# Attention and channel mixing on one core: x as the stationary operand of the token mix, the query scale inside the row maximum, weight conversion's last addition on VectorE

## The chip, the cores and the metric

The kernel runs on one core of one Trainium2 chip. The metric is the device time of an execution in microseconds (us), lower is better; a kernel's time is the median of its runs. Engine names are those of the profile: PE is the matrix engine's multiplications and PEld its loads of stationary operands, DVE is VectorE, ACT is ScalarE, POOL is GpSimd, and SP only issues transfers.

## The reference

```python
# attention: q, k, v are (4 batches, 8 heads, 576 rows, 64); tau = 0.02
scores = q @ k.T / sqrt(64)
thresh = max(scores, -1) - tau
scores = where(scores >= thresh, scores, -1e9)
attn   = exp(scores - max(scores, -1))
attn   = attn / (sum(attn, -1) + 1e-9)
x      = attn @ v                       # heads side by side: (4, 576, 512)
# token mix (rank 32) and channel layers
h   = x.transpose(0, 2, 1) @ U @ V      # U (576, 32), V (32, 576)
u   = x + h.transpose(0, 2, 1)
x   = u + relu(u @ w_ch1) @ w_ch2       # w_ch1 (512, 2048), w_ch2 (2048, 512)
# gated convolution over rows, 5 taps
gate = sigmoid(sum_k conv_w[k] * x shifted by 4 - k rows)
out  = (gate * (x @ w_val)) @ w_out
```

The weights arrive as 64-bit floats; the kernel reads them as pairs of 32-bit words and converts them itself.

## The kernel before, in words

**Precision.** A product that must be as good as 32-bit is made of three products of a faster type: an operand is split into a high part (a copy on ACT) and a low part (a subtraction on DVE or POOL), and high x high, high x low and low x high are summed. Transposes and the products with the values and with U stay in plain 32-bit, in which one product is issued as two instructions.

**Attention: 16 pairs of heads, nine slots each.** A head has 576 rows, four tiles of 128 and a tail of 64. The two tails of a pair share slot 0, the eight tiles are slots 1 to 8. The loop over s in `attention` issues in every slot: `soft_max` (DVE, one pass over the scores in PSUM that writes their negatives `ns` and takes their minimum `nm`), `soft_exp` (ACT, and a one-column sum `th` on POOL), `soft_mask` of the slot before (DVE: keeps what is above the threshold and sums it), then on PE the scores of the next slot (`scores`, two buffers in PSUM) and the transposes of the slot before the last (`trans_main`, `trans_tail`), whose results ACT copies out. `pv` multiplies by the values (twice in a pair), `back` transposes the result back, and a DVE multiplication by 1/sum writes x into `ring`. `mix_t` then makes t = x^T U, `mix_u` and `mix_ut` make u = x + t V. `prep_T` and `stacks` prepare q and k of the next pair. What ACT and DVE do with a PE result is put off with `later(slot, place)`: place 0 and 1 come before `soft_exp`, 2 and 3 behind it. `ORDER` sorts the PE work of a slot, `LATE_ORDER` what is put off, `AT` and `PREP_AT` say in which slot of a pair a step falls.

In `mix_t` the stationary operand is `u4`, U repeated four times (128 columns), and x moves (128 columns), five products, so that t comes out four times one above the other (128 x 128); a copy and a subtraction in the lower half make the high and low parts.

**Weight conversion.** `from_f64` turns a 128 x 512 block into 32-bit in seven steps: absolute value (ACT), clamp, shift, merge, mask, scaled low word (DVE) and one last addition (POOL). The steps are generators; `Staged.tick` moves up to `width` blocks one step on, and each call of `tick` stands at a fixed place of the program. Ten blocks are converted during attention (U, V, and the first quarter of both channel weights, `chunk(0, 0)` and `chunk(0, 1)`), the rest between matrix products afterwards. The queue of each engine is in order: a step waits there and holds up what is behind it.

**After attention.** The first quarter of the channel layers runs straight (`h1`, `ch`, blocks of 512 rows). Beside it `combos` forms sums and differences of blocks of u in `ring`, splits them into three landing tiles in `c_sb` and writes them to DRAM. The other three quarters (c = 1 to 3) use a seven-product scheme: `first_layer` fetches seven operands from DRAM (`region`), multiplies them (lines 1163) and combines the results in `c_sb` on DVE (lines 1139, 1151, and 1134 for the low parts); `second_layer` (1201) adds into u (1204). The weights of the next quarter are combined on DVE (202) and split on ACT and POOL (208, 209) meanwhile. `val` and `proj` are the gated convolution's products and the output.

Of the kernel before, what the change touches and what calls it, by code (L numbers as in the profile page):

```python
# [36 lines left out]
def attention_moe_kernel(  # L37
# [15 lines left out]
    nc = tc.nc  # L53
# [44 lines left out]
    def from_f64(dst, t, raw, clp=0, lowp=0):  # L98
# [30 lines left out]
        nc.gpsimd.tensor_tensor(out=dst, in0=dst, in1=tf, op=ALU.add)  # L129
# [16 lines left out]
    def convert(raw, clp=0, lowp=0, into=None):  # L146
# [7 lines left out]
        yield from from_f64(w[0:m, 0:n], t[0:m, 0:n], raw, clp, lowp)  # L154
# [61 lines left out]
    class Staged:  # L216
# [21 lines left out]
        "pv": (8, 12), "back": 13, "t": 15, "u": 18, "lq": 0, "lv": 4, "uv": 4, "ch": 10,  # L238
    }

    PREP_AT = {"Tq": (-3, 0), "Tk": (1, 1), "Tt": (2, 2), "stA": (4, 4), "bd": (4, 4), "stB": (5, 5)}

    ORDER = {
        "mix_t": 4, "mix_u": 3, "mix_ut": 5, "next_scores": 0, "prep_T": 5, "pv": 3, "back": 2,
        "trans_main": 2, "trans_tail": 2,
    }
    LATE_ORDER = {
        "T": -2, "n": -1, "nt": -2, "o": -1, "t": 0, "u": 1, "x": -2,
    }

    CONVERT_AT = (0, 1, 6, 9, 12, 16)
# [14 lines left out]
    def attention(dense_front, dense_mid, dense_top, dense_left, dense_back):  # L266
# [15 lines left out]
        u4 = setup.tile([128, 5, 128], F32, name="u4")  # L282
# [24 lines left out]
        def load_qk(p):  # L307
            eng = nc.gpsimd if 1 < p < 4 else nc.sync
# [47 lines left out]
        def hi_lo_qk(p, nm, ps, a, n):  # L356
            qk = st8[p]["qk"]
            hi = qk[:, {"q": 0, "k": 1}[nm], a:a + n]
            lo = qk[:, {"q": 3, "k": 2}[nm], a:a + n]

            def act():
                if nm == "q":
                    nc.scalar.activation(out=hi, in_=ps, func=ACTF.Copy, scale=qscale[:, 0:1])
                else:
                    nc.scalar.activation(out=hi, in_=ps, func=ACTF.Copy)

            def dve():
                if nm == "q":
                    nc.vector.scalar_tensor_tensor(
                        out=lo, in0=ps, scalar=qscale[:, 0:1], in1=f(hi), op0=ALU.mult, op1=ALU.subtract  # L370
                    )
                else:
                    nc.vector.tensor_tensor(out=lo, in0=ps, in1=f(hi), op=ALU.subtract)

            return act, dve


        def hi_lo_q0(hh, dst, ps):
# [3 lines left out]
                lambda: nc.scalar.activation(out=hi, in_=ps[a], func=ACTF.Copy, scale=qscale[a, 0:1]),  # L382
                lambda: nc.vector.scalar_tensor_tensor(
# [919 lines left out]
```

## Time and profile before

| | |
|---|---|
| median of 3 runs | 816.7 us (813.84 to 816.81) |
| the profiled execution: time, span | 815.51 us, 813.7 us |
| PE, PEld busy, share of the span | 98%, 89% |
| DVE, ACT, POOL busy | 84%, 54%, 31% |
| granted clock of the matrix engine | 0.999 of full speed (2.4 GHz) |

Busy time of PE includes the modelled ends of pipelined products, so that a busy PE may still have been held up for a part of it; what the matrix engine issues is seen from the starts of its instructions. The span is cut below into startup (0 to 28 us), attention in its steady state (28 to 312), the first quarter of the channel layers (312 to 424), the other three (424 to 711) and the end.

### The profile page before, as it was taken

To read this page: it belongs to the slowest core of one execution; us is meant where nothing else is said; L and a number is where in the kernel's file an instruction comes from. 1 tells how busy PE (TensorE), PEld (TensorE's weight loads), DVE (VectorE), ACT (ScalarE), POOL (GpSimd) and SP (SyncE) were. 2 spreads that over 40 slices of the span, in tenths; PEclk is the share of its full clock that TensorE was granted. 3 is DMA by queue.
4 is the path that set the end of the run, shared out by engine and by line. 5 is a ranking of instruction groups with operands and counts; after the bars stand their busy time and mean duration, and the time that the engine had idled before them with its cause. 6 is when DMAs were issued, how large, how long until landed. Compare 5 with 4: busy or idle time off the path is not lost.

```text
span 813.7 us, 15121 instructions
## 1 busy us (share of the span) xinstructions
PE 798.9 (98%) x5264; PEld 721.0 (89%) x5264; DVE 680.1 (84%) x1426; ACT 442.1 (54%) x929; POOL 252.3 (31%) x350
## 2 busy tenths in 40 slices
PE   9999999999999999999999999999999999999998
PEld 8788888888888887888799998998999999988886
DVE  7999999999999997387989799588899898988740
ACT  6789888888898887343433225132243252355431
POOL 6723622632422331044353226311464230000000
PEclk9999999999999999999999999999999999999999
DMA  5666776685676443445768658277475573001112
GB/s 152 182 143 147 177 166 150 140 203 134 144 183 143 103 104 137 147 153 207 287 247 301 209 216 298 73 303 263 152 297 200 214 272 116 2 1 52 52 53 77
DMA packets 87397, 134.19 MB, mean 165 GB/s; under 512 B 45669, under 2 KB 62837, under 8 KB 87322
## 3 DMA queue, kind: packets, MB, share of 16 engines
q1 hardware_dynamic: 85130, 130.92, 52.7%
q0 software_dynamic: 848, 1.92, 0.8%
q8 instruction: 42, 0.69, 0.3%
q10 hardware_dynamic: 1344, 0.39, 0.2%
q14 instruction: 33, 0.27, 0.1%
HBM read 85.43 MB, written 21.23 MB: 131 GB/s over the span
## 4 chain that ended last, share of the span: by engine, by line
PE 81%; DVE 8%; DMA 4%; issue 2%; ACT 2%; POOL 1%; ACTq 0%; DVEq 0%; POOLq 0%; SPq 0%
PE s L469 9%; PE o L578 8%; PE c L1201 8%; PE a L1201 8%; PE xm L524 7%; PE v L913 6%; PE p L1101 6%; PE a L1163 5%; PE c L1163 5%; PE a L913 4%; PE c L913 3%; DMA region<-sp 2%; PE o L567 2%; PE t L617 2%; DMA sp<-c_sb 2%
## 5 line engine op out<-in xcount | busy, mean ns | idle before, releaser
L508 DVE SCALAR_TENSOR_TENSOR e<-ns,th,e 128x576 f32<-128x576 f32 x144 | 124.4, 864 | 1.5 <-POOL th L498 0.4
L498 POOL TENSOR_TENSOR th<-nm,scalars 128x1 f32<-128x1 f32 x144 | 70.2, 487 | 178.1 <-DVE ns L483 171.1
L497 ACT ACTIVATE e<-ns,nm 128x576 f32<-128x576 f32 x144 | 111.9, 777 | 20.4 <-DVE ns L483 20.3
L483 DVE TENSOR_SCALAR_CACHE_REDUCE ns<-s 128x576 f32<-128x576 f32 x144 | 107.7, 748 | 9.0 <-PE s L469 8.2
L129 POOL TENSOR_TENSOR wf<-wf,wt 128x512 f32<-128x512 f32 (+2 forms) x43 | 59.9, 1394 | 134.1 <-DVE wt L124 131.0
L469 PE MATMUL s<-st 128*128 128x288 f32 x480 | 94.0, 318 | 0.1
L524 PE MATMUL xm<-idn,e 128*128 128x128 f32 x576 | 86.6, 273 | 2.4 <-DVE e L508 2.4
L533 ACT ACTIVATE pt<-xm 128x512 f32<-128x512 f32 x144 | 85.7, 595 | 1.6
L1201 PE MATMUL a<-region,w 128*128 128x384 f32 x432 | 80.9, 334 | 1.0 <-DVE region L1134 1.0
L1201 PE MATMUL c<-region,w 128*128 128x384 f32 x432 | 80.7, 334 | 0.0
L1163 PE MATMUL a<-region,w_s 128*128 128x384 f32 x378 | 76.6, 337 | 2.9 <-DVE c_sb L1139 1.5
L469 PEld LDWEIGHTS s<-st 128*128 128x128 f32 x480 | 67.8, 189 | 11.9 <-issue 4.6
L1201 PEld LDWEIGHTS a<-region,w 128*128 128x128 f32 x432 | 75.3, 188 | 1.3 <-DVE region L1134 1.3
L1163 PE MATMUL c<-region,w_s 128*128 128x384 f32 x378 | 75.7, 334 | 0.0
L1201 PEld LDWEIGHTS c<-region,w 128*128 128x128 f32 x432 | 75.4, 188 | 0.0
L524 PEld LDWEIGHTS xm<-idn,e 128*128 128x128 f32 x576 | 69.4, 141 | 4.6 <-PE s L469 2.3
L1140 ACT ACTIVATE region<-c_sb 128x384 fp32r<-128x384 f32 x72 | 37.7, 525 | 64.6 <-DVE c_sb L1139 64.3
L1163 PEld LDWEIGHTS a<-region,w_s 128*128 128x128 f32 x378 | 65.8, 188 | 5.3 <-DVE c_sb L1139 3.1
L578 PE MATMUL o<-pt,vt 128*64 128x256 f32 (+1 forms) x768 | 69.8, 331 | 0.0
L1163 PEld LDWEIGHTS c<-region,w_s 128*128 128x128 f32 x378 | 66.4, 188 | 0.0
L578 PEld LDWEIGHTS o<-pt,vt 128*64 128x64 f32 x768 | 41.4, 137 | 24.4 <-issue 10.6
L172 ACT ACTIVATE w<-wf 128x512 fp32r<-128x512 f32 x28 | 17.7, 631 | 66.4 <-POOL wf L129 66.4
(164 smaller groups left out, 1555.7 us busy)
## 6 DMA issues: line engine op xcount, KB each, us to landing
region<-sp SPq DMA_DIRECT2D x63, 768.0 KB, 6.0
raw<-in_moe_w_ch_dram SPq DMA_DIRECT2D x32, 512.0 KB, 4.5
sp<-c_sb SPq DMA_DIRECT2D x24, 384.0 KB, 2.9
st<-qk SPq DMA_DIRECT2D x30, 256.0 KB, 3.4
st<-qk SPq DMA_DIRECT2D x15, 432.0 KB, 3.9
st<-qk SPq DMA_DIRECT2D x45, 144.0 KB, 3.9
out_dram<-c_sb SPq DMA_DIRECT2D x17, 256.0 KB, 2.0
st<-qk SPq DMA_DIRECT2D x15, 288.0 KB, 4.9
```

The lines of the kernel that those rows point to most:

```text
L129: nc.gpsimd.tensor_tensor(out=dst, in0=dst, in1=tf, op=ALU.add)
L469: nc.tensor.matmul(s[:, n, 0:HS], lhs, rhs[:, n * HS:(n + 1) * HS], start=(m == 0), stop=(m == len(ops) - 1))
L483: nc.vector.tensor_scalar(out=ns.rearrange("p (a b) -> p a b", a=2), in0=s, scalar1=-1.0, scalar2=3.0e38, op0=ALU.mult, op1=ALU.min, accum ...
L497: nc.scalar.activation(out=row(p, i), in_=d["ns", i], func=ACTF.Exp, bias=nm[:, 0:1], scale=-1.0)
L498: nc.gpsimd.tensor_tensor(out=th, in0=nm, in1=tau_eff, op=ALU.add)
L508: nc.vector.scalar_tensor_tensor(out=e, in0=d.pop(("ns", i)), scalar=d.pop(("th", i))[:, 0:1], in1=e, op0=ALU.is_le, op1=ALU.mult, accum_o ...
L524: nc.tensor.transpose(x[:, j * 128:(j + 1) * 128], e[:, c + j * 128:c + (j + 1) * 128], idn)
L533: later(s + 1, 0, lambda: nc.scalar.activation(out=dst, in_=x.rearrange("p (j c) -> p j c", j=4), func=ACTF.Copy), "x")
L578: nc.tensor.matmul(o, lhs, rhs, start=False, stop=stop)
L913: nc.tensor.matmul(ps[:, 0:m1], lhs, rhs, start=(m == 0), stop=(m == len(ops) - 1))
L1163: nc.tensor.matmul(ps, lhs, rhs, start=k == 0, stop=k == 5)
L1201: nc.tensor.matmul(ps, lhs, rhs, start=k == 0, stop=k == 3 * KD - 1)
```

## The change

- `mix_t`: x is the stationary operand and U (`u1`, 32 columns) moves; t comes out as 128 x 32. ACT copies it twice side by side, DVE subtracts it twice (128 x 64), a new step `mix_tt` transposes the four parts together on PE (128 x 128), and ACT copies the result to `t_st`.
- The query scale is no longer applied to q when its parts are made (plain copy and subtraction), but within `soft_max`: the factor there was the constant -1 and is now a per-partition operand, `qscale`, which holds -1/8.
- `from_f64`: after slot 144, the last addition is on DVE. U and V take their clamp and scaled low word on POOL and ACT and the addition on DVE; the first quarter of both weights takes the scaled low word on DVE (for w_ch1 it was ACT and POOL) and the subtraction for the low part on DVE.
- `soft_mask` moves ahead of the work that is put off; `th` of the first pair moves from POOL to DVE; loads of q and k of pairs 2 and 3 move from POOL's queue to SP's.
- Slots: `mix_t` 15 to 16, `mix_tt` 18, `mix_u` and `mix_ut` 18 to 20, `chunk(0, 0)` 10 to 6, `chunk(0, 1)` 10 to 110; `mix_t`, `mix_tt`, `mix_ut` and the tails' `pv` share a small PSUM tile. The tables of ticks change.
- `combos` has four landing tiles, and from its second third on its differences are on DVE. `fetch` takes free buffers from a list, with as many in flight as before.

```diff
-    def from_f64(dst, t, raw, clp=0, lowp=0):
+    def from_f64(dst, t, raw, clp=0, lowp=0, add=nc.gpsimd):
...
-        nc.gpsimd.tensor_tensor(out=dst, in0=dst, in1=tf, op=ALU.add)
+        (nc.vector if slot[0] > 9 * NP else add).tensor_tensor(out=dst, in0=dst, in1=tf, op=ALU.add)
...
-            eng = nc.gpsimd if 1 < p < 4 else nc.sync
+            eng = nc.sync
...
-                if nm == "q":
-                    nc.scalar.activation(out=hi, in_=ps, func=ACTF.Copy, scale=qscale[:, 0:1])
-                else:
-                    nc.scalar.activation(out=hi, in_=ps, func=ACTF.Copy)
+                nc.scalar.activation(out=hi, in_=ps, func=ACTF.Copy)
...
-                out=ns.rearrange("p (a b) -> p a b", a=2), in0=s, scalar1=-1.0, scalar2=3.0e38, op0=ALU.mult,
+                out=ns.rearrange("p (a b) -> p a b", a=2), in0=s, scalar1=qscale[:, 0:1], scalar2=3.0e38, op0=ALU.mult,
...
-            nc.gpsimd.tensor_tensor(out=th, in0=nm, in1=tau_eff, op=ALU.add)
+            (nc.gpsimd if p or 0 else nc.vector).tensor_tensor(out=th, in0=nm, in1=tau_eff, op=ALU.add)
...
-            x = xtile("t")[:, 0:128]
-            t, xs = t_st[p % 2], x_of(p)
+            x = xsmall(s)[:, 0:R]
+            t, xs = tt_sb[p % 2], x_of(p)
             for j in range(5):
-                nc.tensor.matmul(x, u4[:, j, :], xs[:, j, :], start=(j == 0), stop=(j == 4))
-            later(s + 1, 0, lambda: nc.scalar.activation(out=t, in_=x, func=ACTF.Copy), "t")
+                nc.tensor.matmul(x, xs[:, j, :], u1[:, j, :], start=(j == 0), stop=(j == 4))
+            both = x.unsqueeze(1).to_broadcast([128, 2, R])
+            later(s + 1, 1, lambda: nc.scalar.activation(out=t[:, 0:2, :], in_=both, func=ACTF.Copy), "t")
             later(s + 1, 3, lambda: nc.vector.tensor_tensor(
-                out=t[64:128], in0=x[64:128], in1=f(t[64:128]), op=ALU.subtract
+                out=t[:, 2:4, :], in0=both, in1=f(t[:, 0:2, :]), op=ALU.subtract
             ), "t")
+
+        def mix_tt(s, p):
+            x = xsmall(s)[:, 0:128]
+            nc.tensor.transpose(x, f(tt_sb[p % 2]).rearrange("p g r -> p (g r)"), idn)
+            later(s + 1, 2, lambda: nc.scalar.activation(out=t_st[p % 2], in_=x, func=ACTF.Copy), "t")
...
-            w = yield from convert(raw_uv[part])
+            w = yield from convert(raw_uv[part], 1, 1, nc.vector)
...
-            if s == AT["ch"]:
-                chunk(0, 0)
-                chunk(0, 1)
-            work.width = 2 if s < 9 * NP - 11 else 4
+            if s == 6: chunk(0, 0)
+            if s == 110: chunk(0, 1)
+            work.width = 2 if s < 9 * NP - 9 else 4
...
-                    if 1 <= s <= 9 * NP:
-                        soft_mask(*divmod(s - 1, 9))
+                if m == 1 and live:
+                    soft_exp(p, i)
+                if m == 0 and 1 <= s <= 9 * NP:
+                    soft_mask(*divmod(s - 1, 9))
...
-              nc.vector if c == 0 and part else nc.gpsimd,
-              *((0, 1) if c == 0 and not part else ())))
+              (nc.vector if part else nc.vector) if c == 0 else nc.gpsimd,
+              *(((0, 0, nc.gpsimd) if part else (0, 0, nc.gpsimd)) if c == 0 else ())))
...
-        outs = [p1["c"][:, 2 * n * G:2 * (n + 1) * G].rearrange("p (a n) -> p a n", a=2) for n in range(3)]
+        outs = [p1["c"][:, 2 * n * G:2 * (n + 1) * G].rearrange("p (a n) -> p a n", a=2) for n in range(4)]
...
-            (nc.vector if j > 1 else nc.gpsimd).tensor_tensor(out=lots[i % 3], in0=x, in1=y, op=ALU.subtract)
+            (nc.vector if j > 0 else nc.gpsimd).tensor_tensor(out=lots[i % 3], in0=x, in1=y, op=ALU.subtract)
...
+        FIRST_TICKS, SECOND_TICKS = [1, 1, 1, 1, 1, 2, 1], [1, 1, 3, 1, 2, 2, 2, 2]
...
-                for _ in range(1):
+                for _ in range(FIRST_TICKS[i]):
                     work.tick()
...
-                    for _ in range(2):
+                    for _ in range(SECOND_TICKS[(1 - half) * KD + e]):
                         work.tick()
```

**PE, around the token mix of one pair** (s are scores, xm and xs transposes, tm the transposes of q or k, o the product with the values), before and then with the change:

```order
L469 MATMUL s<-st 128x288 x4
L524 MATMUL xm<-idn,e 128x128 x4
L541 MATMUL xs<-idn,e 128x128
L617 MATMUL t<-ring,u_139 128x128 x5
L396 MATMUL tm<-idn,qn 128x128 x4
L469 MATMUL s<-st 128x288 x4
L524 MATMUL xm<-idn,e 128x128 x4
L469 MATMUL s<-qk,bd_144 128x288 x6
```

```order
L453 MATMUL s<-st 128x288 x4
L601 MATMUL xs<-u_139,ring 128x32 x5
L508 MATMUL xm<-idn,e 128x128 x4
L453 MATMUL s<-qk,bd_146 128x288 x6
L508 MATMUL xm<-idn,e 128x128 x4
L525 MATMUL xs<-idn,e 128x128
L551 MATMUL xs<-pk_1307,vk_153 128x64
L551 MATMUL o<-pk,vk_153 128x256
L562 MATMUL xs<-pt_1304,vt_151 64x64 x8
L562 MATMUL o<-pt,vt_151 64x256 x8
L453 MATMUL s<-st 128x288 x4
L610 MATMUL xs<-idn,tt_sb_140 128x128
```

The five products stand one slot later and are 32 columns wide; the new transpose stands two slots behind them, after the products with the values.

**DVE, the same stretch of a pair** (ns is the pass over the scores, e the mask, qk the low part of q, t_st and tt_sb the low part of t), before and then with the change:

```order
L483 TENSOR_SCALAR ns,nm<-s 128x576
L603 TENSOR_TENSOR ring<-b,r 128x512
L508 SCALAR_TENSOR_TENSOR e,sum<-ns,th,e 128x576
L483 TENSOR_SCALAR ns,nm<-s 128x576
L508 SCALAR_TENSOR_TENSOR e,sum<-ns,th,e 128x576
L483 TENSOR_SCALAR ns,nm<-s 128x576
L508 SCALAR_TENSOR_TENSOR e,sum<-ns,th,e 128x576
L369 SCALAR_TENSOR_TENSOR qk<-tm,scalars,qk 128x512
L619 TENSOR_TENSOR t_st_147<-t,t_st_147 64x128
```

```order
L467 TENSOR_SCALAR ns,nm<-s,scalars 128x576
L492 SCALAR_TENSOR_TENSOR e,sum<-ns,th,e 128x576
L587 TENSOR_TENSOR ring<-b,r 128x512
L467 TENSOR_SCALAR ns,nm<-s,scalars 128x576
L492 SCALAR_TENSOR_TENSOR e,sum<-ns,th,e 128x576
L467 TENSOR_SCALAR ns,nm<-s,scalars 128x576
L492 SCALAR_TENSOR_TENSOR e,sum<-ns,th,e 128x576
L359 TENSOR_TENSOR qk<-tm,qk 128x512
L467 TENSOR_SCALAR ns,nm<-s,scalars 128x576
L492 SCALAR_TENSOR_TENSOR e,sum<-ns,th,e 128x576
L604 TENSOR_TENSOR tt_sb_141<-xs,tt_sb_141 128x64
```

The mask comes directly behind the pass over the scores in every slot, and the pass reads a per-partition operand; the query's subtraction no longer does.

**DVE, a first layer of the seven-product scheme** (c_sb are the sums, region the low parts, wt and wf a weight block under conversion), before and then with the change:

```order
L1134 SCALAR_TENSOR_TENSOR region<-c_sb,region 128x384
L124 SCALAR_TENSOR_TENSOR wt<-raw,wt 128x512
L103 TENSOR_SCALAR wt<-wt 128x512
L1139 TENSOR_TENSOR c_sb<-a,c_sb 128x384
L1134 SCALAR_TENSOR_TENSOR region<-c_sb,region 128x384
L1139 TENSOR_TENSOR c_sb<-c,c_sb 128x384
L1134 SCALAR_TENSOR_TENSOR region<-c_sb,region 128x384
L106 TENSOR_SCALAR wt<-wt 128x512
```

```order
L124 SCALAR_TENSOR_TENSOR wt<-raw,wt 128x512
L103 TENSOR_SCALAR wt<-wt 128x512
L1130 TENSOR_TENSOR c_sb<-a,c_sb 128x384
L1125 SCALAR_TENSOR_TENSOR region<-c_sb,region 128x384
L1130 TENSOR_TENSOR c_sb<-c,c_sb 128x384
L1125 SCALAR_TENSOR_TENSOR region<-c_sb,region 128x384
L129 TENSOR_TENSOR wf_5428<-wf_5428,wt 128x512
L106 TENSOR_SCALAR wt<-wt 128x512
L110 SCALAR_TENSOR_TENSOR wf_5428<-raw,wt 128x512
```

The addition (line 129) stands between two of the layer's own steps, where it was POOL's before.

## Rows read from the trace of the kernel before

**Rows 1.** Busy time by stretch: us, busy of PE, PEld, DVE, ACT, POOL, clock, DMA

```profile
28.00:312.00 284.00, 281.95 (x2437) 243.45 (x2437) 267.31 (x697) 244.25 (x569) 109.03 (x218) 1.00 0.62 146
312.00:424.00 112.00, 109.98 (x572) 91.17 (x573) 82.37 (x127) 45.33 (x89) 40.64 (x32) 1.00 0.58 202
424.00:711.00 287.00, 283.17 (x1623) 280.17 (x1622) 247.66 (x446) 93.69 (x166) 83.71 (x60) 1.00 0.59 211
```

**Rows 2.** Waits of PE: line, waited for, us in total, times, longest

```profile
PE xm L524 <- DVE e L508: 2.4, 5, 0.6
PE s L469 <- DVE ns L483: 0.8, 1, 0.8
PE a L913 <- DVE region L847: 2.0, 3, 1.1
PE a L1163 <- DVE c_sb L1139: 1.5, 2, 0.7
PE a L1201 <- DVE region L1134: 1.0, 1, 1.0
```

**Rows 3.** The chain that ended last: first product with the values of four pairs

```profile
47.93 2.34 PE o L578 x32
...
238.23 2.35 PE o L578 x32
...
257.03 2.34 PE o L578 x32
...
295.36 2.34 PE o L578 x32
```

**Rows 4.** Timeline of PEld: start, us; products of 64, 128 and 128 columns follow

```profile
15.06 0.53 PEld L462 LDWEIGHTS s<-qk,st 128*128 128x128 f32 x4
...
119.20 1.20 PEld L617 LDWEIGHTS t<-ring,u 128*128 128x128 f32 x10
...
120.32 0.47 PEld L396 LDWEIGHTS tm<-idn,qn 128*128 128x128 f32 x4
```

**Rows 5.** DVE by line and shape: count, busy us, mean ns, idle before

```profile
L483 DVE TENSOR_SCALAR_CACHE_REDUCE ns<-s 128x576 f32<-128x576 f32 x144 | 107.7, 748 | 9.0 <-PE s L469 8.2
L1134 DVE SCALAR_TENSOR_TENSOR region<-c_sb,region 128x384 fp32r<-128x384 f32 x72 | 45.2, 627 | 0.6 <-ACT region L1140 0.6
...
L1139 DVE TENSOR_TENSOR c_sb<-c,c_sb 128x384 f32<-128x384 f32 x36 | 19.6, 546 | 0.1
...
L369 DVE SCALAR_TENSOR_TENSOR qk<-tm,scalars,qk 128x512 fp32r<-128x512 f32 x15 | 11.2, 747 | 2.4 <-ACT qk L363 2.2
L373 DVE TENSOR_TENSOR qk<-tm,qk 128x512 fp32r<-128x512 f32 x16 | 11.0, 690 | 4.6 <-ACT qk L365 4.6
...
L619 DVE TENSOR_TENSOR t_st<-t,t_st 64x128 fp32r<-64x128 f32 x16 | 4.7, 295 | 0.5
...
L174 DVE TENSOR_TENSOR w<-wf,w 128x512 fp32r<-128x512 f32 x4 | 2.7, 684 | 0.0
```

**Rows 6.** POOL by line and shape: the last addition of a conversion

```profile
L129 POOL TENSOR_TENSOR wf<-wf,wt 128x512 f32<-128x512 f32 x41 | 57.6, 1405 | 123.4 <-DVE wt L124 120.3 <-ACT region L924 3.1
```

**Rows 7.** The mask's line: duration in ns, shortest, median, longest

```profile
L508 DVE SCALAR_TENSOR_TENSOR e<-ns,th,e x144: 800/814/1678, 12.3 to 313.0; 128x576 f32<-128x576 f32 x144
```

**Rows 8.** Timeline of all engines around 98 us: start, us, idle before

```profile
97.90 1.28 POOL L174 TENSOR_TENSOR w<-wf,w 128x512 fp32r<-128x512 f32 x1
...
98.12 1.68 DVE L508 SCALAR_TENSOR_TENSOR e<-ns,th,e 128x576 f32<-128x576 f32 x1
...
99.95 0.63 PE L524 MATMUL xm<-idn,e 128*128 128x128 f32 x4 [0.57 <-DVE e L508]
```

**Rows 9.** The chain from 350 to 395 us: a landing tile's transfer

```profile
361.33 7.33 DMA sp<-c_sb
```

**Rows 10.** DVE's timeline in the same stretch: the split of a block of u

```profile
388.20 2.88 DVE L847 TENSOR_TENSOR region<-u,region 128x512 fp32r<-128x512 f32 x2
```

**Rows 11.** The chain in a first layer: six products of 384 columns

```profile
456.55 1.04 PE c L1163 x6
```

More of the change, by code (lines that the diff above doesn't have):

```diff
@@ L280, in attention @@
         s_ps = ps_s.enter_context(tc.tile_pool(name="s_ps", bufs=2, space=PSUM))
-        u4 = setup.tile([128, 5, 128], F32, name="u4")
+        u1 = setup.tile([128, 5, R], F32, name="u1")
+        tt_sb = [setup.tile([128, 4, R], F32R, name=f"tt_sb{i}") for i in range(2)]
         vst = setup.tile([128, S], F32R, name="vst")
@@ L565, in pv @@
                 pt = d.pop(("pt", g))
-                o = xtile("o")
+                o = xtile("o") if g else xsmall(s)
                 nc.tensor.matmul(
@@ L707, in setup_UV @@
             done.append(0)
-        NS = 9 * NP + AT["u"] - 7
-        slots = [[] for _ in range(NS + 1)]
+        NS = 9 * NP + 12
+        slots = [[] for _ in range(NS + 40)]
         def put(s, what, *a):
@@ L720, in attention @@
                     put(s0 + i + 2, trans_tail, p, i)
-            put(s0 + AT["pv"][0], pv, p, 0, 1)
-            put(s0 + AT["pv"][1], pv, p, 2)
-            put(s0 + AT["back"] + end, back, p)
+            put(s0 + 8, pv, p, *(0, 1))
+            v2 = s0 + (13 if end else 12)
+            put(v2, pv, p, *(2,))
+            put(v2 + 1, back, p)
             if p + 1 < NP:
-                for name, what, *a in (("Tq", prep_T, "q"), ("Tk", prep_T, "k"), ("Tt", prep_T, "tail"),
-                                       ("stA", stacks, 0), ("bd", tails), ("stB", stacks, 1)):
-                    put(s0 + PREP_AT[name][not p], what, p + 1, *a)
-            put(s0 + AT["t"], mix_t, p)
-            put(s0 + AT["u"] - end, mix_ut, p)
-            put(s0 + AT["u"] - end, mix_u, p)
+                for what, at, *a in ((prep_T, (-3, 0), "q"), (prep_T, (1, 1), "k"), (prep_T, (2, 2), "tail"),
+                    (stacks, (3, 5), 0), (tails, (4, 5)), (stacks, (5, 3), 1)):
+                    put(s0 + at[not p], what, p + 1, *a)
+            put(s0 + (15 if end else 16), mix_t, p)
+            put(s0 + (17 if end else 18), mix_tt, p)
+            put(s0 + (18 if end else 20), mix_ut, p)
+            put(s0 + (18 if end else 20), mix_u, p)
         def next_scores(s):
@@ L778, in attention @@
                 dense_mid()
-            if s == 9 * NP + AT["back"] + 1 - 9:
+            if s == 9 * NP + 5:
                 top.close()
@@ L1115, in proj, with fetch @@
                 tick(2)
+        FIRST_TICKS, SECOND_TICKS = [1, 1, 1, 1, 1, 2, 1], [1, 1, 3, 1, 2, 2, 2, 2]
         operands = [region(n * 1536, 1536).rearrange("p (a k n) -> p a k n", a=2, k=2) for n in range(4)]
         hs = region(6144, 6144).rearrange("p (a k n) -> p a k n", a=2, k=KD)
-        stream = [(c, j, o) for c in range(1, NCH) for j in range(NG) for o in ORDER_OF]
-        fetched, used = [], [0]
-        def fetch(n):
-            while len(fetched) < min(n, len(stream)):
-                _, j, o = stream[len(fetched)]
-                t = operands[len(fetched) % 4]
-                nc.sync.dma_start(out=f(t), in_=spilled[j, o])
+        stream = [(j, o) for c in range(1, NCH) for j in range(NG) for o in ORDER_OF]
+        fetched, free = [], operands[0:2]
+        def fetch():
+            while stream:
+                if not free:
+                    return
+                t = free.pop(0)
+                nc.sync.dma_start(out=f(t), in_=spilled[stream.pop(0)])
                 fetched.append(t)
@@ L1231, in dense @@
         lot(100)
+        free.extend(operands[2:])
         p1.pop("lots")
@@ L1234, in dense @@
             ch(0, *held.pop(0))
+        work.width = 4
         for c in range(1, NCH):
```

70 lines of the change are left out of this document (27 added, 43 removed).

## The prediction

> **What bounds the kernel now.** I read the busy times by stretch first [rows 1], then what PE waited for [rows 2], then the chain that ended last [rows 3, 9, 11], and at last DVE and POOL by shape. PE is busy 281.95 of 284.00 us in the steady part of attention, 109.98 of 112.00 in the first quarter of the channel layers and 283.17 of 287.00 in the other three [rows 1]; the clock is at its upper level (2.4 GHz) throughout. So nothing is gained by making another engine's work shorter, unless PE waits for that piece of it. The waits are few: 2.4 us for the mask, 0.8 for the pass over the scores, 2.0 for a split of u, 1.5 and 1.0 for a sum and a low part in the three later quarters [rows 2], 7.7 us in all. The rhythm of attention tells the same: one undisturbed pair takes 257.03 − 238.23 = 18.80 us, thirteen such would take 244.4, and the thirteen from 47.93 to 295.36 took 247.43 [rows 3]. Hence 3.0 us are lost there. DVE is second: 267.31 of 284.00 is 17.7 us in a pair of 18.8 [rows 1], a cover of 1.1 us in a pair. The profiled execution took 815.51 us, 1.2 under the median 816.7 of the three runs; all sums start from it.
>
> **The change part by part.**
>
> *Token mix.* Five products of 128 columns become five of 32; each is issued as two instructions. What does such a pair cost? Four products with 64 columns moving show their loads from first to last in 0.53 us, ten with 128 columns in 1.20, four transposes in 0.47 [rows 4]. The first two fit one line: one less than the count times 0.112 us, and 0.19 for the last load. So the price per instruction is that of its load, whether 64 or 128 columns move, and the load keeps its 128 x 128 shape when x is stationary. I take 0 for the narrowing. The other end is that the columns do set a part of the price: 96 columns fewer at 2.4 GHz are 40 ns, for 160 instructions (16 pairs, ten each) 6.4 us less; row 64 against row 128 is the nearest and speaks for 0. The Trainium skill ("TensorE: Matmul & The Clock Gate", section "Back-to-back issue gap") gives a narrow product an issue floor of about 25 ns; by that, 160 x (112 − 25) ns = 13.9 us would go, as an estimate from the page. Its next section, on loading the stationary operand, gives 128 columns / 1.2 = 107 ns, and the row's 112 agrees with that one.
>
> The new transpose adds one load and product to each pair: (0.47 − 0.14)/3 = 0.11 us by the transposes [rows 4], 16 of them +1.7 us. It waits for nothing, since it stands two slots behind the products, with the products with the values between. Its copy goes to ACT, which has 40 us to spare in the stretch [rows 1].
>
> *Query scale.* DVE's subtraction with a per-partition factor took 747 ns, without one 690, on the same 128 x 512 shape [rows 5]. So the factor costs 57 ns. It is added to 144 passes of 748 ns [rows 5], +8.2 us of DVE, 0.5 in a pair, and taken from the query's subtractions, −0.9. The low part of t, 295 ns on 64 x 128 [rows 5], becomes 128 x 64 and about 80 ns shorter. Net +0.4 us per pair. Nothing hides that but the 1.1 us of cover, which it fits into; the ends are 0 (should the factor be free in this kind of instruction) and, if the cover is not where it is wanted, 13 x 0.4 = 5 us.
>
> *Mask and conversions in attention.* Why the mask is late is seen at 98 us: it takes 1.68 us where its median is 814 ns [rows 7, 8], beside a POOL subtraction of 128 x 512 that lies over it, and PE's transposes then wait 0.57 [rows 8]. Three of the five waits for the mask are of this kind, 1.7 of 3.0 us. With the change the second set of weight blocks enters conversion at slot 110 instead of 10, and POOL has 7 of the 128 x 512 two-input operations among the slots instead of 17; the middle pairs keep none at all on DVE either, which pays for the 0.4. The mask also comes ahead of everything that is put off, so a late ACT step can't hold it. I take 2.4 of the 3.0. The Trainium skill ("GPSIMD Engine Reference", section "Key points") says that GpSimd shares its SBUF interfaces with VectorE and contends with instructions that have two SBUF inputs; the 1.68 agrees. By that rule the moved additions, which have two SBUF inputs on DVE themselves, would now be the ones that collide with POOL's remaining subtractions: that is rival C.
>
> *Startup.* The five waits for the mask minus the three leave 0.7, and the one for the pass over the scores is 0.8 [rows 2]: 1.5 us. U's and V's conversion on three engines, q and k of pairs 2 and 3 on another queue, `th` of the first pair on DVE: none of these shows a price of its own before. What is queued behind the loads on SP are the transfers of the first pairs' parts, which could come later by one transfer. I take 0.8 of the 1.5, with 1.5 less and 1 more as the ends.
>
> *Landing tiles.* In the first quarter a transfer out of a landing tile took 7.33 us [rows 9]. With three tiles the split that should fill the fourth waits for it at the head of DVE's queue, and behind it stands the split of u that PE wants, which ended only at 388.20 + 2.88 us [rows 10]: PE lost 2.0 [rows 2]. With a fourth tile that wait moves one block later, and by then the transfer is over. I take 1.8 of 2.0; the end on the other side is that the same queue is stopped by ten additions at 0.684 [rows 5] = 6.8 us new on DVE in this stretch, which has 112.00 − 82.37 = 29.6 to spare [rows 1]. So 0 to 2.0.
>
> *Last addition after attention.* POOL needed 1,405 ns [rows 6]; DVE needs 684 for a subtraction of this shape [rows 5]. By the order 24 go to DVE in the three later quarters: 16.4 us more on 247.66 of 287.00 [rows 1], 264 in all, still under. POOL's additions overlap DVE's work, and the low parts that run beside them are slower than the sums, 627 against 546 ns [rows 5] on one shape: 72 x 81 ns = 5.8 us of DVE come back in part. Where it counts is a first layer. There PE takes fourteen groups of 1.04 us [rows 11] = 14.6, and DVE its 14 sums and 8 low parts of 0.546 = 12.0 plus conversion steps: by the order 0 to 3.4 us before, 1.0 to 4.1 after. Only four of the 24 additions fall into first layers; the rest fall into second layers, where DVE has little else. I take 0.8 of the 2.5 us of waits [rows 2] as gone; ends 2.5 less and, in rival C, much more.
>
> Sum: startup −0.8, attention −2.4, transposes +1.7, landing tiles −1.8, last addition −0.8: −4.1 us. 815.51 − 4.1 = **811.4 us**.
>
> **The rivals.**
>
> *A, the stalls change place.* The relief in attention is eaten by the slower pass over the scores, and the first quarter's queue waits for another transfer. For it: DVE has only 1.1 us of cover in a pair. Against: in the middle pairs DVE loses its conversion steps. Then startup and landing tiles give half, −1.3, the transposes cost 1.7: 815.9 us, no change that can be told.
>
> *B, the narrow products are cheap.* The columns count after all, 6.4 less: 811.4 − 6.4 = 805.0 us. Against it stands the 64-column row.
>
> *C, DVE becomes what PE waits for in the first layers.* At 12.0 + 4.1 = 16.1 DVE is over PE's 14.6; it decides from 2.6 us of conversion steps on. Seven of nine first layers have such steps; at 0.8 each, 5.6 us. If half of the 24 additions also collide with a POOL subtraction and PE waits for each what it waited for the mask at 98 us, 0.57 [rows 8], that is 6.8 more. With the gains before 424 us kept: 815.5 − 3.3 + 12.4 = 824.6 us. For it: before, a first layer's waits for sums and low parts are already the only ones in the stretch. Against: only four additions lie there, and POOL's own collisions go.
>
> **How the numbers follow.** About 0.5% (4.1 us, hence 812.6 and 820.8) is what a measurement of this kernel can tell from no change. Forecast 0.54, A 0.26, B 0.08, C 0.12. The forecast's own range, with the ends above, is 808 to 815: nearly three quarters of it lie under 812.6, 0.39 of faster, with B 0.47. Same: 0.15 from the forecast and 0.24 of A. Slower: C and a little of A. Range 804 to 817: it holds the forecast, nearly all of A and the upper half of B, and leaves out C and the rest of B.
>
> **What would show it.** Right: the first product with the values comes every 18.9 us (18.80 + 0.11) in all middle pairs; the ten loads of the mix still span about 1.2 us; the pass over the scores takes about 805 ns; the masks of over 1.5 us are gone; no wait of PE for the split of u at 390 us. Wrong: loads of the mix in 0.6 us (B); a pair of 19.2 us with PE waiting for the pass over the scores (A, or the factor dearer than 57 ns); waits of PE for sums and low parts growing from 2.5 us to 8 and more (C); a new wait of PE around 314 us, where two conversions now stand among the first splits.

## The result, and the profile after

The changed kernel takes 808.2 us (median of 4 executions, 807.9 to 808.7) against 816.5 us before (4 executions, 813.8 to 816.8): ratio 0.990, 95% interval 0.988 to 0.992, 8.3 us less. The profiled executions differ by 815.51 − 807.92 = 7.6 us. For two experiments below (e_loads, e_chunk) the profiled execution ran at a lowered clock (0.556 and 0.753); their traces are not used, and their times are over the other executions.

Where the 7.6 us lie is read from the starts of the same products in both timelines. First the kernel before, where [rows 3] do not show it: the first product with the values, that of the last pair (the chain in [rows 3] has each such start 0.07 later), the first product of the later quarters' first layers, and the first behind them. Columns are start, duration of the group (us), engine, line, operation.

```profile
28.61 1.77 PE L578 MATMUL o<-pt,vt 128*64 128x64 f32 x26
...
295.29 1.98 PE L578 MATMUL o<-pt,vt 128*64 128x64 f32 x28
...
423.69 1.21 PE L1163 MATMUL a<-region,w_s 128*128 128x384 f32 x6
...
711.27 2.01 PE L913 MATMUL v<-region,w 128*128 128x512 f32 x8
```

The same places after (45.29 and 290.31 answer to the first and the last of [rows 3]):

```profile
26.59 0.69 PE L562 MATMUL xs<-pt,vt 128*64 128x64 f32 x16
...
45.29 0.69 PE L562 MATMUL xs<-pt,vt 128*64 128x64 f32 x16
...
64.12 0.69 PE L562 MATMUL xs<-pt,vt 128*64 128x64 f32 x16
...
83.40 0.69 PE L562 MATMUL xs<-pt,vt 128*64 128x64 f32 x16
...
234.13 0.69 PE L562 MATMUL xs<-pt,vt 128*64 128x64 f32 x16
252.95 0.69 PE L562 MATMUL xs<-pt,vt 128*64 128x64 f32 x16
271.79 0.69 PE L562 MATMUL xs<-pt,vt 128*64 128x64 f32 x16
290.31 0.69 PE L562 MATMUL xs<-pt,vt 128*64 128x64 f32 x16
...
417.55 1.21 PE L1154 MATMUL a<-region,w_s 128*128 128x384 f32 x6
...
703.61 1.55 PE L902 MATMUL v<-region,w 128*128 128x512 f32 x6
```

| stretch | lead at its end, us | gained in it | predicted |
|---|---|---|---|
| startup, to the first product with the values | 2.0 | 2.0 | 0.8 |
| attention, to 290.31 | 295.29 − 290.31 = 5.0 | 3.0 | 0.7 (2.4 − 1.7) |
| handover and first quarter | 6.1 | 1.2 | 1.8 |
| three later quarters | 7.7 | 1.5 | 0.8 |
| the rest | 7.6 | −0.1 | 0 |

Not all of the startup's 2.0 us is the change's. The first scores start at 8.43 us before and at 8.01 after,

```profile
8.43 1.04 PE L469 MATMUL s<-qk,bd 128*128 128x288 f32 x6
```

```profile
8.01 1.05 PE L453 MATMUL s<-qk,bd 128*128 128x288 f32 x6
```

and in the twelve traces of this document that start lies between 7.99 (b_loads, nearly the kernel before) and 8.69 us (e_add, up to there the changed kernel), so 0.4 of the 2.0 can be chance. From the first scores to the first product with the values it is 28.61 − 8.43 = 20.18 us before and 26.59 − 8.01 = 18.58 after, 1.6 less.

The thirteen pairs of [rows 3], 247.43 us, now take 290.31 − 45.29 = 245.02; an undisturbed one 252.95 − 234.13 = 18.82 instead of 18.80. What PE waits for after, by line, releaser, us in total, times and longest, answers to [rows 2]:

```profile
PE a L1154 <- DMA region<-sp: 1.8, 4, 0.9
...
PE a L902 <- DVE region L836: 0.8, 2, 0.6
PE s L453 <- DVE ns L467: 0.4, 1, 0.4
...
PE a L1154 <- DVE region L1125: 0.2, 1, 0.2
```

The waits for the mask (2.4) are gone altogether, those for sums and low parts (1.5 and 1.0) fell to 0.2, that for the split of u from 2.0 to 0.8. The operands' transfers, 0.9 before, took 1.8. The busy times of [rows 1] after, for the steady part and the later quarters:

```profile
28.00:312.00 284.00, 283.59 (x2470) 245.32 (x2466) 260.35 (x700) 241.96 (x584) 114.64 (x203) 1.00 0.62 145
...
424.00:711.00 287.00, 284.74 (x1621) 280.29 (x1620) 253.28 (x467) 94.71 (x167) 44.23 (x31) 1.00 0.56 203
```

In attention DVE (fifth number) went down from 267.31 to 260.35 although its pass grew; in the quarters it took over 5.6 us while POOL (seventh) halved. The rows of DVE and POOL that answer to [rows 5 to 7], by line and shape (count, busy us, mean ns), and the lines of the mask and of the last addition on DVE (shortest, median, longest):

```profile
L467 DVE TENSOR_SCALAR_CACHE_REDUCE ns<-s,scalars 128x576 f32<-128x576 f32 x144 | 116.9, 812 | 18.1 <-PE s L453 17.5
L1125 DVE SCALAR_TENSOR_TENSOR region<-c_sb,region 128x384 fp32r<-128x384 f32 x72 | 43.5, 604 | 2.4 <-ACT region L1131 2.3
```

```profile
L492 DVE SCALAR_TENSOR_TENSOR e<-ns,th,e x144: 803/815/1243, 11.3 to 308.9; 128x576 f32<-128x576 f32 x144
L129 DVE TENSOR_TENSOR wf<-wf,wt x37: 389/684/1661, 29.9 to 648.0; 128x512 f32<-128x512 f32 x35, 128x224 f32<-128x224 f32 x1, 5x512 f32<-5x512 f32 x1
```

The longest mask is 1,243 ns instead of 1,678; the pass costs 812 ns instead of 748.

### The profile page after: what moved, and what is told of

It reads as the page before. It is cut to its first block, busy times and chain, and to the rows that moved or that the text cites. A ratio compares the mean times of both kernels' runs of the same rounds, so it can differ in the third digit from the quotient of the medians.

```text
span 805.8 us, 15115 instructions
## 1 busy us (share of the span) xinstructions
PE 796.4 (99%) x5280; PEld 720.1 (89%) x5280; DVE 684.9 (85%) x1484; ACT 438.5 (54%) x943; POOL 198.2 (25%) x280
## 4 chain that ended last, share of the span: by engine, by line
PE 91%; DVE 4%; DMA 4%; issue 1%; SPq 0%; ACT 0%; DVEq 0%; ACTq 0%
PE s L453 10%; PE a L1192 9%; PE c L1192 9%; PE xm L508 7%; PE o L562 7%; PE a L1154 6%; PE v L902 6%; PE a L902 6%; PE c L902 6%; PE p L1090 6%; PE c L1154 6%; DMA region<-sp 3%; PE xs L601 2%; PE o L551 2%; PE tm L380 2%; PE xs L562 1%
## 5 line engine op out<-in xcount | busy, mean ns | idle before, releaser
L467 DVE TENSOR_SCALAR_CACHE_REDUCE ns<-s,scalars 128x576 f32<-128x576 f32 x144 | 116.9, 812 | 18.1 <-PE s L453 17.5
L482 POOL TENSOR_TENSOR th<-nm,scalars 128x1 f32<-128x1 f32 x135 | 86.5, 641 | 161.3 <-DVE ns L467 158.4
L492 DVE SCALAR_TENSOR_TENSOR e<-ns,th,e 128x576 f32<-128x576 f32 x144 | 119.3, 828 | 0.0
L174 POOL TENSOR_TENSOR w<-wf,w 128x512 fp32r<-128x512 f32 x20 | 29.0, 1448 | 164.7 <-ACT w L172 155.7
L562 PE MATMUL o<-pt,vt 128*64 128x256 f32 x512 | 61.5, 382 | 0.0
L562 PEld LDWEIGHTS o<-pt,vt 128*64 128x64 f32 x512 | 34.0, 137 | 19.2 <-issue 5.3
L1090 PE MATMUL p<-w,region 128*128 128x512 f32 x216 | 49.6, 389 | 0.0
```

What stands on the lines that cost most here:

```text
L467: nc.vector.tensor_scalar(out=ns.rearrange("p (a b) -> p a b", a=2), in0=s, scalar1=qscale[:, 0:1], scalar2=3.0e38, op0=ALU.mult, op1=ALU. ...
L482: (nc.gpsimd if p or 0 else nc.vector).tensor_tensor(out=th, in0=nm, in1=tau_eff, op=ALU.add)
L492: nc.vector.scalar_tensor_tensor(out=e, in0=d.pop(("ns", i)), scalar=d.pop(("th", i))[:, 0:1], in1=e, op0=ALU.is_le, op1=ALU.mult, accum_o ...
L562: nc.tensor.matmul(o, lhs, rhs, start=False, stop=stop)
L1090: nc.tensor.matmul(ps, t[:, a, kk, sl], w[:, bb, kk, :], start=(m == 0), stop=(m == 3 * KD - 1))
```

## The experiments

Most take one part of the change back and leave the rest; the changed kernel's 808.2 us (807.9 to 808.7) is what they are read against. Two traces of the same program differ too: up to the first product with the values e_add and e_tiles issue what the changed kernel issues, and reach it 0.5 and 0.05 us after 26.59; and the waits for `region<-sp` run from 0.7 to 4.9 us over the traces below. The three later quarters, 703.61 − 417.55 = 286.1 us in the changed kernel, took 284.2 in e_mix and 288.8 in e_best, whose edits lie in attention alone:

```profile
417.44 0.86 PE L1152 MATMUL a<-region,w_s 128*128 128x384 f32 x4
...
701.61 1.09 PE L900 MATMUL v<-region,w 128*128 128x512 f32 x4
```

```profile
417.10 1.21 PE L1162 MATMUL a<-region,w_s 128*128 128x384 f32 x6
...
705.89 1.31 PE L910 MATMUL v<-region,w 128*128 128x512 f32 x5
```

So up to 0.7 us that stands before the first scores, and up to 4 us in the later quarters, is not read from one pair of traces; the steady rhythm of attention is read to 0.01 us a pair. The times of one kernel scatter by 0.7 us in some of these runs and by 3.5 in others, so a difference of 1 to 1.5 us between medians of four is near the limit of what they can tell.

**e_loads**: loads of pairs 2 and 3 on POOL's queue again.

```diff
-            eng = nc.sync
+            eng = nc.gpsimd if 1 < p < 4 else nc.sync
```

> The changed kernel with one part undone: the loads of q and k of pairs 2 and 3 are issued from POOL's queue again. Theory (POOL's queue is the startup's stall: its issues of about 0.8 us stand ahead of th, for which the mask waits): the first product with the values comes 1 us or more later than the changed kernel's 26.6 us, and the time is 809.2 to 810.2 us. Rival (the loads are hidden, the startup's gain is from the conversion of U and V): first product within 0.3 us of 26.6, time 808.2 with 0.4 either way.

Measured: 809.8, 810.8 and 811.0 us, 2.5 more than the changed kernel. The time is over the theory's upper end, 810.2; where it is lost can't be shown without a trace.

**b_loads**: the kernel before, with this part alone.

```diff
-            eng = nc.gpsimd if 1 < p < 4 else nc.sync
+            eng = nc.sync
```

> The kernel before with one part of the change alone: the loads of q and k of pairs 2 and 3 go through SP's queue instead of POOL's. With the part undone the changed kernel lost 2.5 us. Theory (POOL's issues, eight of about 0.75 us, stand ahead of th in the first two pairs, and that is the startup's stall): the first product with the values comes 1 to 2 us before 28.6 us, time 1.5 to 2.5 us under the kernel before. Rival (it is a gain only together with the other moves of the startup, since th is still on POOL): within 0.3 us of 28.6, time within 0.7 us of the kernel before.

Measured: 815.4 us (10 executions) against 816.2 (14), ratio 0.9993 with the interval 0.9983 to 1.0004. The products with the values start at 28.1 instead of 28.6:

```profile
L578 PE MATMUL o<-pt,vt x30: 222/270/382, 28.1 to 29.9; 128*64 128x64 f32 x16, 128*64 128x256 f32 x14
```

Of these 0.5 us, 0.4 stands before the first scores (7.99 us here, 8.43 before); from there it is 20.1 us against 20.2. The rival was right in the time: the move is worth 2.5 us inside the changed kernel and nothing that can be told by itself. That it is the other moves of the startup that need it is likely, but which of them is not shown.

**e_uv**: conversion of U and V as before.

```diff
-            w = yield from convert(raw_uv[part], 1, 1, nc.vector)
+            w = yield from convert(raw_uv[part])
```

> The changed kernel with one part undone: U and V are converted as before (clamp and scaled low word on DVE, last addition on POOL). Theory (conversion's DVE steps stand ahead of the first pairs' passes and masks): the first product with the values comes 1 us or more after 26.6 us, time 809.2 to 810.2 us. Rival (the startup's gain is from the loads or from the place of the mask): within 0.3 us of 26.6, time 808.2 with 0.4 either way.

Measured: 809.6 us (808.5 to 811.0). The first product comes 0.3 us late, as the rival said, but behind it PE waits for a mask (at 35.9 us), and for the pass three times in all instead of once (the last at 146):

```profile
PE s L453 <- DVE ns L467: 1.1, 3, 0.5
PE xm L508 <- DVE e L492: 1.0, 1, 1.0
```

By the times the part is worth about 1.4 us. The trace, taken from the slowest of the four executions (811.0), is late by 0.3 us at the first product with the values, where the theory had looked, by 2.0 at the second pair's first and by 3.0 at the last pair's:

```profile
47.29 0.69 PE L562 MATMUL xs<-pt,vt 128*64 128x64 f32 x16
...
293.27 0.69 PE L562 MATMUL xs<-pt,vt 128*64 128x64 f32 x16
```

So in that execution taking this part back lost 2.6 us in attention, nearly what the table above has as gained there.

**e_mask**: the mask behind the exponential again.

```diff
-                if m == 0 and 1 <= s <= 9 * NP:
+                if m == 1 and 1 <= s <= 9 * NP:
                     soft_mask(*divmod(s - 1, 9))
```

> The changed kernel with one part undone: the mask of the slot before stands behind the exponential and the work put off before it, as it did. Theory (its earlier place shields the mask from late steps): PE waits for the mask or the pass, 0.5 to 2 us more, time 808.7 to 810.2. Rival (the long masks were POOL's doing, the place does nothing): time 808.2 with 0.4 either way.

Measured: 809.5 us (808.4 to 810.1), 1.3 more. Its first products with the values, of the first pair and near the end, stand at

```profile
27.78 0.69 PE L562 MATMUL xs<-pt,vt 128*64 128x64 f32 x16
...
291.67 0.69 PE L562 MATMUL xs<-pt,vt 128*64 128x64 f32 x16
```

that is 1.2 us after the changed kernel's at the first and 1.4 at the last. Half of the 1.2 stands before the first scores (8.60 us against 8.01) and can be chance; 0.6 is the startup's, where the mask is waited for again (0.4 us). Behind it only 0.2 us more is lost up to the last pair, so in the steady part its place does next to nothing; the trace is from the fastest of the four executions, and the rest of the 1.3 is not placed.

**e_chunk, e_chunk2**: the second set of weight blocks from slot 10 (twice the same kernel).

```diff
-            if s == 110: chunk(0, 1)
+            if s == 10: chunk(0, 1)
```

> The changed kernel with one part undone: the second set of weight blocks enters conversion at slot 10 again instead of 110. Theory (POOL's 128 x 512 two-input operations beside a mask are what made attention stall): three or more masks of over 1.5 us in the steady part come back, PE waits 0.5 to 0.6 us for each, and the time is 809.5 to 811. Rival (the mask's earlier place in the slot hides a long mask): the long masks come back but PE waits for none of them, time 808.2 with 0.4 either way.

> The changed kernel once more with the second set of weight blocks in conversion from slot 10, for its trace: the time was 811.5 us against 808.2. Theory (POOL's 128 x 512 operations beside masks): masks of over 1.5 us between 45 and 290 us with waits of PE behind them make up 2 us or more of the 3.3. Rival (DVE's own conversion steps in the middle pairs, which now lack the cover): pairs get longer with no long mask, PE waiting for the pass over the scores.

Measured: 811.5 us (median of four, 810.7 to 813.6), and 812.7 (811.7 to 812.8): 3.3 to 4.5 us more. But the mask's line reads

```profile
L492 DVE SCALAR_TENSOR_TENSOR e<-ns,th,e x144: 802/815/1230, 11.4 to 313.3; 128x576 f32<-128x576 f32 x144
```

No long mask came back, and between 28 and 312 us PE waits neither for a mask nor for the pass. Both theories fall. One wait holds 2.1 us, and the chain of waits names a transfer of V that took 6.39 us, issued 1.5 us behind a weight block, with the stacked operands of the scores behind it on the same queue (timeline of PE, then chain):

```profile
240.67 1.30 PE L453 MATMUL s<-st 128*128 128x288 f32 x4 [2.11 <-DMA qn<-in_q_dram]
```

```profile
230.12 6.39 DMA vt<-in_v_dram
```

Between the first product of this pair (234.88) and that of the next (257.60) lie 22.72 us instead of 18.82. The late entry keeps the weights' transfers away from the middle pairs' own: this is read from one trace and has no run of its own.

**e_wide**: the narrow products made wide.

```diff
-            x = xsmall(s)[:, 0:R]
+            xw = xsmall(s)
+            x = xw[:, 0:R]
...
-                nc.tensor.matmul(x, xs[:, j, :], u1[:, j, :], start=(j == 0), stop=(j == 4))
+                nc.tensor.matmul(xw.rearrange("p (g r) -> p g r", g=4), xs[:, j, :],
+                    u1[:, j, :].unsqueeze(1).to_broadcast([128, 4, R]), start=(j == 0), stop=(j == 4))
```

> The changed kernel with the five products of the token mix moving U four times side by side (128 columns instead of 32; three quarters of the result are not read). If the load alone sets the price, nothing changes (808.2 with 0.4 either way, and the ten instructions start 0.112 us apart). By the changed kernel's trace nine of ten starts follow at 0.112 us and one at 0.03 after; if that one is won by the narrow product, the wide one loses 0.08 us in each of 16 pairs, 1.3 us: 809.5.

Measured: 808.9 us (808.3 to 809.5). The loads of the ten instructions take 1.23 us from the first to the end of the last in the changed kernel, with 32 columns, and 1.21 here, with 128 (timelines of PEld, one line of each kernel):

```profile
117.38 1.23 PEld L601 LDWEIGHTS xs<-u,ring 128*128 128x128 f32 x10
```

```profile
118.03 1.21 PEld L602 LDWEIGHTS xs<-u,ring 128*128 128x128 f32 x10
```

Ten pairs (the first products with the values at 64.69 and 253.91) take 189.22 us; in the changed kernel, 64.12 to 252.95, 188.83. So 0.04 us in a pair, 0.6 in all: the price is the load's, and only the follower of the last product starts sooner. The 1.3 expected took that start's whole 0.08 for a gain.

**e_mix**: the old token mix in the new slots.

```diff
-                nc.tensor.matmul(x, xs[:, j, :], u1[:, j, :], start=(j == 0), stop=(j == 4))
+                nc.tensor.matmul(x, u4[:, j, :], xs[:, j, :], start=(j == 0), stop=(j == 4))
...
-            put(s0 + (17 if end else 18), mix_tt, p)
```

(and one copy to `t_st` and one subtraction in its lower half, as before)

> The changed kernel with one part undone: U four times side by side is stationary and x moves, one copy and one subtraction make the parts of t, and the transpose of t is gone; the slots are the changed kernel's. Theory (only PE's instructions count): 0.107 us of transpose go and 0.07 us of products come back in each of 16 pairs, 0.6 us less, 807.6 us with 0.4 either way. Rival (the new form saves PE time or waits that the count does not show): 808.9 or more.

Measured: 807.2 us (805.7 to 809.0). Two pairs ten apart, here and in the changed kernel (there at 83.40 and 271.79):

```profile
84.19 0.69 PE L561 MATMUL xs<-pt,vt 128*64 128x64 f32 x16
...
271.98 0.69 PE L561 MATMUL xs<-pt,vt 128*64 128x64 f32 x16
```

187.79 against 188.39 us: 0.06 us in a pair, 1.0 in sixteen. The theory holds: the new mix costs PE about 1 us, and buys nothing that shows.

**e_scale**: the query scale on q, the constant -1 in the pass.

```diff
-                out=ns.rearrange("p (a b) -> p a b", a=2), in0=s, scalar1=qscale[:, 0:1], scalar2=3.0e38, op0=ALU.mult,
+                out=ns.rearrange("p (a b) -> p a b", a=2), in0=s, scalar1=-1.0, scalar2=3.0e38, op0=ALU.mult,
```

(and the scale in q's copies and subtractions, as before)

> The changed kernel with one part undone: the query scale is applied when q's parts are made, and the factor of the pass over the scores is the constant -1. Theory (DVE's cover in a pair hides the factor): the pass takes 748 instead of 812 ns, DVE has 0.4 us less in a pair, PE's rhythm stays at 18.83 us, time 808.2 with 0.4 either way. Rival (the dearer pass is on the path): a pair shorter by 0.1 to 0.4 us, time 802 to 807.

Measured: 808.2 us (806.9 to 810.1), no difference. The pass:

```profile
L477 DVE TENSOR_SCALAR_CACHE_REDUCE ns<-s 128x576 f32<-128x576 f32 x144 | 108.1, 751 | 20.8 <-PE s L463 20.7
```

751 against 812 ns, 0.5 us of DVE in a pair, all hidden.

**e_add**: the last addition on POOL after slot 144.

```diff
-        (nc.vector if slot[0] > 9 * NP else add).tensor_tensor(out=dst, in0=dst, in1=tf, op=ALU.add)
+        add.tensor_tensor(out=dst, in0=dst, in1=tf, op=ALU.add)
```

> The changed kernel with one part undone: the last addition of a conversion stays on POOL after slot 144 too. Theory (POOL's additions make DVE's low parts slow and late): waits of PE for sums and low parts come back, 0.8 to 2.5 us, time 809.0 to 810.7. Rival (the 24 additions cost DVE more than they give): waits of PE in the three later quarters fall, and the time is 1 us or more under the changed kernel's 808.2.

Measured: 808.5 us (807.8 to 808.6), 0.3 more, inside the scatter. The low parts are slower again, and one is waited for:

```profile
L1125 DVE SCALAR_TENSOR_TENSOR region<-c_sb,region 128x384 fp32r<-128x384 f32 x72 | 45.4, 630 | 5.8 <-ACT region L1131 5.8
```

```profile
PE a L1154 <- DVE region L1125: 1.6, 1, 1.6
```

630 against 604 ns shows the mechanism of the theory, but PE's time hardly feels it. The rival (DVE overloaded by the additions) is out.

**e_tiles**: three landing tiles.

```diff
-        outs = [p1["c"][:, 2 * n * G:2 * (n + 1) * G].rearrange("p (a n) -> p a n", a=2) for n in range(4)]
+        outs = [p1["c"][:, 2 * n * G:2 * (n + 1) * G].rearrange("p (a n) -> p a n", a=2) for n in range(3)]
```

> The changed kernel with one part undone: three landing tiles for the sums of blocks of u instead of four. Theory (a transfer of several us out of the third-last tile holds up DVE's queue): PE waits again for the split of u in the first quarter, 1.2 to 2.0 us more, time 809.4 to 810.2. Rival (the first quarter gained by its new order of conversion steps): no new wait, time 808.2 with 0.4 either way.

Measured: 809.6 us, all four executions between 809.2 and 809.9: 1.4 more, the size expected. The split of u runs at its usual length with three tiles, but 1.3 us later (382.65 in the changed kernel), and PE's loads wait for it once more, at the place that the theory named:

```profile
383.99 1.29 DVE L836 TENSOR_TENSOR region<-u,region 128x512 fp32r<-128x512 f32 x2 [0.23 <-ACT region L835]
```

```profile
384.73 1.38 PEld L902 LDWEIGHTS a<-region,w 128*128 128x128 f32 x11 [0.42 <-DVE region L836]
```

From the last pair's first product with the values (290.34) to the first product of the later quarters (418.01) it takes 127.67 us, 0.4 more than the changed kernel's 127.24. So the wait expected is there, but with 0.4 us instead of 1.2 to 2.0. What else is longer in this trace lies in the later quarters, within what traces differ by; where the rest of the 1.4 us is saved stays open.

**e_best**: old mix and old scale together.

> The changed kernel with two parts undone: the old token mix (U four times, stationary, no transpose) and the query scale on q with a constant -1 in the pass over the scores. By the two single runs, 1.0 us less for the mix and nothing for the scale: 807.2 us. Rival (the two share their gain of cover with other parts, or the mix's 1.0 was chance, by the count 0.6): 807.6 to 808.2.

Measured: 807.3 us (806.6 to 810.1), ratio to before 0.989 (0.987 to 0.990). The best median is e_mix's; with the scatter of either it can't be told from the changed kernel by its times alone, only by its rhythm.

## Why the prediction was right, and where its steps failed

The sign and the range held, but the range, 804 to 817 us, is so wide that no change at all, 816.5, would have lain in it too. The size was short, 4.1 us against 7.6 on the profiled executions: the terms of attention and of the startup were too small, and some stood on the wrong edit.

*Attention, 0.7 taken, 3.0 measured.* This is the largest miss of the sum. From the first product with the values to the last pair's stand fourteen pairs: 266.68 us before, 3.5 more than 14 undisturbed ones of 18.80, and 263.72 after, 0.2 more than 14 of 18.82. So 3.2 us of stalls went where 2.4 were taken, and the rhythm grew by 0.3 where 1.7 were taken for the transposes (against the old mix in the same slots by 1.0, e_mix).

*Startup, 0.8 taken, 2.0 measured.* Without what can be chance it is 1.6, from the first scores on. The step that failed is the share, half of the 1.5 us that the waits of [rows 2] give, and that they were taken as a cap: between the first scores and the first product with the values PE's named waits are 0.18, 0.81 and 0.46 us before, 0.38 and 0.21 after. They fell by 0.9 us, and the stretch by 1.6. Taken back one by one, the parts cost 1.4 (U and V), 1.3 (place of the mask) and 2.5 us (loads), though of the first two only 0.2 and 0.6 stand in this stretch; their sum is over what was gained, and the loads alone give nothing. How they act together is not shown, and `th` of the first pair on DVE, which could hold a share, was not taken back. The mask's place had been booked under attention, where it does next to nothing.

*Long masks.* That they were POOL's doing and would go was right: none over 1.25 us is left and PE waits for none. That slot 110 was the reason was wrong: with slot 10 they stay away. Between 40 and 308 us POOL had 16 additions and subtractions of 128 x 512 before, in three groups:

```profile
L129 POOL TENSOR_TENSOR wf<-wf,wt 128x512 f32<-128x512 f32 x8 | 11.8, 1473 | 0.0
L122 POOL TENSOR_TENSOR wt<-raw,wt 128x512 f32<-128x512 f32 x4 | 5.8, 1440 | 0.0
L174 POOL TENSOR_TENSOR w<-wf,w 128x512 fp32r<-128x512 f32 x4 | 5.7, 1413 | 0.0
```

After there are six, and eight in e_chunk2, all of the first kind. Nor is it the mask's place: in e_mask the longest is 1.17 us. So what is left is the scaled low word and the low part on DVE, and where the remaining additions now begin; the two were not run apart. The late entry is worth 3 to 4 us for another reason, by e_chunk2's one trace the transfers, which the prediction did not look at.

*Transposes, +1.7, and narrow products, 0.* Measured for the whole new mix is 1.0 us of cost (e_mix), of which narrowing gives back 0.6 (e_wide): so 1.6 for the transposes, nearly the 1.7 taken, and 0.6 less for the narrowing, which was taken at 0. Rival B, 6.4 us, is out by a factor of ten.

*Query scale.* 57 ns predicted, 61 measured (812 − 751), hidden as said.

*First quarter, 1.8 taken, 1.2 measured.* This pair of traces may flatter it: b_loads, whose program is that of the kernel before in this stretch, takes 422.06 − 294.41 = 127.65 us for the stretch, where the kernel before took 128.40 and the changed kernel 127.24. The waits behind 388 us (1.12 and 0.43) went. The landing tiles have a share in that, but the prediction had the wrong queue: what waited for a tile's transfer was ACT's copy, with ACT's half of the split of u behind it,

```profile
387.12 0.53 ACT L885 ACTIVATE c_sb<-ring 128x384 fp32r<-128x384 f32 x1 [3.04 <-DMA sp<-c_sb]
```

and with three tiles in the changed kernel only 0.4 us of wait comes back (e_tiles). The larger share is the length of the split: the prediction did not ask why two splits that take 1.29 us after took 2.88 before [rows 10]. The row that tells stood on POOL, where `combos` formed its differences:

```profile
387.96 2.57 POOL L882 TENSOR_TENSOR ring<-u 128x384 f32<-128x384 f32 x2 [1.91 <-DVE c_sb L890]
```

It lies over most of the split, 387.96 to 390.53 against 388.20 to 391.08. After, the second third's differences are on DVE, and the split takes 1.29 us, with three tiles as with four. The diff had that line; the prediction gave it no price. That this line and no other did it was not run apart.

*Last addition, 0.8 taken.* The mechanism was seen (604 against 630 ns), the gain is 0.3 us and within the scatter. The three later quarters gained 1.5 us in the traces, which is less than traces of the same program differ by there. Rival C is out: the 24 additions found room (four of them ran into a POOL subtraction, where C had twelve), and the waits for sums and low parts fell.

Rival A is out too: the rhythm of a pair stayed at 18.82, under the 18.9 of the forecast's signals and far from the 19.2 of A's, the pass came to 812 ns (about 805 said), and the small new wait that was named for 314 us is there, 0.8 us in two pieces.

## What to carry to other kernels

A cap on what a stretch can give back must not be taken from its waits with a named releaser: in the startup these fell by 0.9 us and the stretch by 1.6. A part that is worth 2.5 us inside a bundle can be worth nothing alone, so each part must be priced with the others in place. Before a gain is read from a pair of traces, see how much traces of one program differ over the same stretch. When an instruction takes twice its usual time, look at what the neighbour engine runs over the same microseconds, and not only at the queue and its transfers. A part of a bundle that adds instructions to the busiest engine (here the transpose) is worth taking back by itself: the rest of the bundle can hide its cost in the total.

## What the runs showed of the hardware

A mask and a large POOL operation do not slow each other by a share; they take turns, whole instructions at a time. Before (two rows), and after, where POOL's operation began earlier under the mask's start (two rows), timelines of POOL and DVE, start and duration:

```profile
288.37 1.28 POOL L129 TENSOR_TENSOR wf<-wf,wt 128x512 f32<-128x512 f32 x1
288.59 1.68 DVE L508 SCALAR_TENSOR_TENSOR e<-ns,th,e 128x576 f32<-128x576 f32 x1
```

```profile
296.54 1.28 POOL L129 TENSOR_TENSOR wf<-wf,wt 128x512 f32<-128x512 f32 x1
...
297.19 1.24 DVE L492 SCALAR_TENSOR_TENSOR e<-ns,th,e 128x576 f32<-128x576 f32 x1
```

POOL keeps its 1.28 us in both, and the mask ends 0.62 and 0.61 us after POOL's end: 290.27 − 289.65 and 298.43 − 297.82, as at 98 us [rows 8], 99.80 − 99.18 = 0.62. Alone the mask takes 0.81, so it is held up by what was left of POOL's operation when it began, less 0.2 us (1.68 − 0.81 = 0.87 against 1.06 left; 1.24 − 0.81 = 0.43 against 0.63). The other way round it holds for POOL's one-column sum, whose shortest is 0.19 us, and which takes 0.63 when a mask has begun before it:

```profile
295.72 0.82 DVE L492 SCALAR_TENSOR_TENSOR e<-ns,th,e 128x576 f32<-128x576 f32 x1
295.95 0.63 POOL L482 TENSOR_TENSOR th<-nm,scalars 128x1 f32<-128x1 f32 x1 [0.85 <-DVE ns L467]
```

It ends at 296.58, the mask at 296.54. A large operation of POOL is held up in the same way: the subtraction at 161.83 us before took 1.80 us, with a mask running from 161.64 to 162.48. The Trainium skill ("GPSIMD Engine Reference", section "Key points") says that the two engines share interfaces and that instructions with two SBUF inputs contend. The rows agree, and here the later one waits for the earlier one's end. The additions that moved to DVE show the same: their median is the 684 ns that an undisturbed operation of this shape takes [rows 5], and the four of 1.32 to 1.66 us each began under a POOL subtraction. The one at 634.08 took 1.60 us and ended 0.57 us after the subtraction that POOL had begun at 633.83.
